# The expert scores of twelve turned columns: from twenty-four matmuls of 128 columns to six of 384

## The chip, the cores and the metric

The kernel runs on one core of one Trainium2 chip. The metric is the device time of one execution in microseconds, taken over repeated runs; the median of three is used. One further execution was recorded by the hardware profiler, and all rows below come from that one.

## What is computed

A sequence of 8 x 2880 tokens of width 192 goes through a short causal convolution with seven taps per head, whose weights are a softmax. Every token is then sent to one of 16 experts (4 groups of 4), a two-layer network with 1024 hidden units, and its output is scaled by the two softmax weights of the choice.

```python
w = softmax(weight_gen)                      # B, S, 8 heads, 7 taps
x = einsum('bshk,bskhg->bshg', w, windows(x_pad))
g_logits = x @ w_group                       # 4 groups
g_idx, g_w = argmax(g_logits), softmax(g_logits)[g_idx]
e_logits = x @ w_expert[g_idx]               # 4 experts of the group
e_idx, e_w = argmax(e_logits), softmax(e_logits)[e_idx]
h = maximum(x @ w1[g_idx, e_idx], 0)
out = g_w * e_w * (h @ w2[g_idx, e_idx])
```

The change concerns the logits alone: the product of every token with the 192 x 20 matrix of the 4 group weights and the 16 expert weights.

## The kernel before

The 23,040 tokens stand as 128 partitions by 180 columns; a *column* below is 128 tokens, one for each partition. The columns are worked in 15 groups of 12 (`WIDTHS`), and a group has two chunks of six. For each group VectorE computes the convolution (`conv`, L317 and L335; in the first six chunks TensorE adds up the products, L358). Then `logits` (L387) scores the group, `ranks` (L450) turns the scores into places in a table of rows, and GpSimd scatters the rows to DRAM (L527). Beside that, once rows are there, blocks of rows of one expert go through the two layers: `gemm1` (L965) and `gemm2` (L1011, later L1013 and L1014), and GpSimd scatters the results (L1049). One *unit* is one `gemm1` and one `gemm2` of an older unit.

The order on TensorE, ScalarE, VectorE and SyncE is the order of the program text as it is generated: a model of the engines' clocks (`clk`, `run`) decides when `step` takes the next piece of a group's work in between units. `run("pe", ...)` in `logits` is the model's cost of the scoring.

Inside `logits` the work of a group is this. Each pair of columns is turned by three transposes (L416, L417): the first 128 of the 192 features of each of the two columns, and the last 64 features of both, stacked on 128 partitions. ScalarE copies the three turned pieces, 384 columns, from PSUM to a tile `xT` (L423), one tile for each pair from a ring of six. `score` then handles two pairs, four token columns j = 0 to 3, with eight matmuls of 128 columns. Each column j has its own strip of 32 columns of the array and 32 partitions of the PSUM tile `lt` (`tile_position=(0, j * LW)`). The first four (u = 0) multiply the 128 features by `wr[:, 0]`, the second four (u = 1) add the product of the stacked 64 features with `wr[:, 1]` or `wr[:, 2]`, which hold the last 64 rows of the weights in the upper or the lower half of the partitions and zeros in the other.

In the groups before `FIRST` = 2 (`early`) a `score` follows each two pairs; from group 2 on all three follow one after another at the end, 24 matmuls. Then ScalarE copies `lt` to `lts` (L435), three transposes turn it back (L443), ScalarE copies the result to `ls` (L446), and `ranks` begins. The PSUM tile `pl` has one buffer, which `lt`, half of the transposes' outputs, `lp` and the ranks' sums use in turn.

Of the kernel before, what the change touches and what calls it, by code (L numbers as in the profile page):

```python
# [9 lines left out]
F32 = mybir.dt.float32  # L10
# [9 lines left out]
WIDTHS = (12,) * 15  # L20
# [22 lines left out]
def conv_moe_kernel(ctx: ExitStack, tc: tile.TileContext, x, wgen, w_group, w_expert, w1, w2, out):  # L43
    nc = tc.nc
# [4 lines left out]
    P = 128  # L49
# [3 lines left out]
    S = NTOK // P  # L53
    PB = P // B
    HALO = K - 1
    SG = 12
    SC = 6
# [14 lines left out]
    ENDS = [r[0] for r in ROUNDS]  # L72
    COL = [sum(WIDTHS[:g]) for g in range(len(WIDTHS) + 1)]
    CHUNK = [c // SC for c in COL]
    assert COL[-1] == S and ENDS[-1] == len(WIDTHS) and all(n % SC == 0 and n <= SG for n in WIDTHS)
    LAG = 2
    TB = 3

# [21 lines left out]
    rt = pool("rt", 1)  # L100
# [36 lines left out]
    ident = const.tile([P, P], F32, name="ident")  # L137
    make_identity(nc, ident)
    tri = const.tile([P, P], BF16, name="tri")
    LW = 32  # L140
    wr = const.tile([P, 3, LW], F32, name="wr")
# [23 lines left out]
    for n in (5, 4, 3, 2, 1):  # L165
        t = const.tile([P, NE], F32, name=f"first{n}")
# [15 lines left out]
    for n in sorted(set(WIDTHS)):  # L182
        t = smask[n] = const.tile([P, NE, n], F32, name=f"smask{n}")
# [70 lines left out]
    def ph_tile(k, shape):  # L254
        return ps_h.tile(shape, F32, name=f"ph{k}")
# [9 lines left out]
    def run(eng, cost, *deps):  # L265
        clk[eng] = max([clk[eng]] + [d + HOP for d in deps]) + cost
        return clk[eng]
# [119 lines left out]
    def logits(g, o):  # L387
        n = WIDTHS[g]
        xrow = o.xrow
        early = g < FIRST  # L390
        pause = lambda t: UNIT if state["begun"] and t > clk["pe"] + 0.9 else NEXT
        yield Chunk(o, 1)
        new_lt = lambda: ps_y.tile([P, SG // 4, P], F32, name="py0") if g == FIRST - 1 else ps_l.tile([P, SG // 4, P], F32, name="pl")
        lt = new_lt() if early else None

        def score(s4, xTs):
            for u in range(2):
                for j in range(2 * len(xTs)):
                    nc.tensor.matmul(  # L399
                        lt[j * LW:(j + 1) * LW, s4 // 4, :], lhsT=wr[:, u * (1 + j % 2), :], rhs=xTs[j // 2][:, (j % 2, 2)[u], :],  # L400
                        start=u == 0, stop=u == 1, tile_position=(0, j * LW))

        xTs, txTs = [], []
        for s2 in range(0, n, 2):
            if o.chunks <= s2 // SC:
                yield Chunk(o, s2 // SC + 1)
            if s2 % SC == 0:
                rem = rt.tile([P, SC, HP], F32, name="rem")
                nc.scalar.copy(out=rem, in_=xrow[s2 // SC][:, :, P:D])
                txTs += [run("act", 0.4, clk["dve"])] * 2  # L410
                yield pause(txTs[-1])
            ttp = run("pe", 0.35, txTs[-2])
            tp = ps_t.tile([P, 3, P], F32, name="tp") if s2 % 4 == 0 else ph_tile(0, [P, 3, P]) if early else ps_l.tile([P, SG // 4, P], F32, name="pl")
            row = xrow[s2 // SC][:, s2 % SC:s2 % SC + 2, :]
            for u in range(2):
                nc.tensor.transpose(out=tp[:, u, :], in_=row[:, u, 0:P], identity=ident)  # L416
            nc.tensor.transpose(out=tp[:, 2, :], in_=rem[:, s2 % SC:s2 % SC + 2, :].rearrange("p s d -> p (s d)"), identity=ident)  # L417
            if early and len(xTs) == 2:
                run("pe", 0.5, txTs[-1])
                score(s2 - 4, xTs)  # L420
                xTs = []
            xT = rt.tile([P, 3, P], F32, name="xT", bufs=SG // 2)
            nc.scalar.copy(out=xT, in_=tp)  # L423
            txTs.append(run("act", 0.48, ttp))
            xTs.append(xT)
            yield NEXT if s2 < n - 2 else pause(txTs[-1])
        lt = lt or new_lt()
        s4 = n - 2 * len(xTs)
        run("pe", 0.1 + 0.2 * len(xTs), txTs[-1])
        for i in range(0, len(xTs), 2):  # L430
            score(s4 + 2 * i, xTs[i:i + 2])
        lts = rt.tile([P, 3, P], F32, name="xT", bufs=SG // 2)
        lps = [(u, min(4, n - 4 * u) * LW) for u in range((n + 3) // 4)]
        if n % 4 == 0:
            nc.scalar.copy(out=lts[:, 0:n // 4, :], in_=lt[:, 0:n // 4, :])  # L435
        else:
            for u, w in lps:
                nc.scalar.copy(out=lts[0:w, u, :], in_=lt[0:w, u, :])
        tlt = run("act", 0.48, clk["pe"])
        yield pause(tlt)  # L440
        lp = ps_l.tile([P, SG // 4, P], F32, name="pl")
        for u, w in lps:
            nc.tensor.transpose(out=lp[:, u, 0:w], in_=lts[0:w, u, :], identity=ident[0:w, 0:w])  # L443
        run("pe", 0.35, tlt)
        ls = rt.tile([P, SG, NL], F32, name="ls")[:, 0:n, :]
        nc.scalar.copy(out=ls, in_=lp.rearrange("p q (j l) -> p (q j) l", l=LW)[:, 0:n, 0:NL])  # L446
        run("act", 0.4, clk["pe"])
        ranking.append([ranks(g, o, ls, Until(clk["act"] + LATE[0 if early else 1])), None])
# [230 lines left out]
    def front():  # L679
# [34 lines left out]
        for g in range(ENDS[-1]):  # L714
            o = grp[g]
            o.routed = False
            scoring.append([logits(g, o), None, o])
            for n, c in enumerate(conv(g, o)):
                yield c
                if g == 0 and n < 6:  # L720
                    for c in islice(rest, None if n == 5 else 1):
                        yield c
                if n == (2 if state["slots"] else 0) and 1 <= g < ENDS[-1] - 1:
                    load_group(g + 1)
                if n >= (12 if state["slots"] or g > FIRST else 4) and not o.ahead and g + 1 < ENDS[-1] and g != FIRST - 1:
                    o.ahead = True
                    side.append([softmax(g + 1), None])
                yield from beside(g, n)
                if g == FIRST - 1 and n in (7, 8):
                    if n == 7:  # L730
                        soft = softmax(FIRST)
                    yield next(soft)
            if g == FIRST - 1:
                for n, c in enumerate(soft):
                    yield c
                    yield from beside(g, n)
            yield from finish_all(side)
            if g:
                yield from settle(g - 1)
# [538 lines left out]
```

## Time and profile before

| | us |
|---|---|
| median of three runs | 1198.86 (1195.1 to 1199.44) |
| profiled execution | 1187.8 |
| its span, first to last instruction | 1185.8 |
| TensorE matmul busy | 1116.4 (94%), 8357 records |
| VectorE busy | 950.8 (80%) |
| ScalarE busy | 649.0 (55%) |
| GpSimd busy | 579.9 (49%) |

Busy time of TensorE is the time in which at least one matmul record is open; records overlap, and their ends are modelled. A matmul of this data type leaves two records, one for each pass, and each has a weight load of its own. "issue" as a reason for idle time means that the engine waited for nothing that the profile shows. In a timeline a row gathers neighbouring instructions of one kind: its start, the time to the end of the last one, their count, and in brackets the idle time ahead of it.

### The profile page before, as it was taken

The numbers are of one execution on the slowest core, as the hardware profiler recorded it, in microseconds if no ns is written. First come the engines' busy times: TensorE is split into PE (matmuls) and PEld (weight loads), VectorE is DVE, ScalarE is ACT, GpSimd is POOL, SyncE is SP. The second block draws the span as 40 slices with busy tenths as digits, with TensorE's granted clock in tenths as the row PEclk, the third lists the DMA queues.
The fourth block names the chain that finished last, engine by engine and source line by source line (L and its number), as shares of the span: only waits on it lengthen the run. The fifth ranks groups of instructions, "written<-read, shape, count | busy, mean of one in ns | idle before, by whom it ended". The sixth has DMA issues, their size and how long they took to land.

```text
span 1185.8 us, 24775 instructions
## 1 busy us (share of the span) xinstructions
PE 1116.4 (94%) x8357; PEld 1047.3 (88%) x8357; DVE 950.8 (80%) x1682; ACT 649.0 (55%) x1307; POOL 579.9 (49%) x613
## 2 busy tenths in 40 slices
PE   5787998999999999999999999999799899999997
PEld 2444988999999999998989999999799899999997
DVE  8899997989998989998988989898464576665661
ACT  1341435555565555665556566565446676666772
POOL 7164284647275745765563837284736421222221
PEclk9998999999999999999999999999999999999999
DMA  5798999887878777878795868767748875556562
GB/s 173 212 310 231 305 310 289 247 276 232 279 228 280 243 256 231 277 224 285 218 304 179 275 214 269 256 197 211 225 134 240 261 243 171 172 182 181 179 208 73
DMA packets 84345, 275.11 MB, mean 232 GB/s; under 512 B 15296, under 2 KB 34160, under 8 KB 82416
## 3 DMA queue, kind: packets, MB, share of 16 engines
q1 hardware_dynamic: 64056, 229.77, 62.3%
q0 software_dynamic: 20032, 43.39, 11.9%
q8 instruction: 67, 1.10, 0.4%
q14 instruction: 70, 0.57, 0.1%
q10 hardware_dynamic: 120, 0.28, 0.1%
HBM read 225.83 MB, written 47.88 MB: 231 GB/s over the span
## 4 chain that ended last, share of the span: by engine, by line
PE 65%; issue 15%; DVE 6%; DMA 4%; POOL 3%; ACT 3%; another core or an unknown queue 2%; SPq 0%; POOLq 0%; ACTq 0%; DVEq 0%
PE py L1011 27%; PE ph L965 27%; POOL out L1049 3%; DVE pr L317 3%; PE pl L399 2%; DMA raw<-in_moe_w 1%; PE tpx L940 1%; PE tpx L939 1%; PE ph L358 1%; PE py L1013 1%; DMA xb<-rows 1%; DVE pr L353 1%; PE tp L416 1%; PE pl L416 1%
## 5 line engine op out<-in xcount | busy, mean ns | idle before, releaser
L965 PE MATMUL ph<-xh,wa 128*128 128x256 f32 (+3 forms) x1992 | 455.0, 303 | 0.4 <-issue 0.3
L1049 POOL DMA_INDIRECT out<-y,xb x189 | 213.8, 1131 | 421.7 <-ACT y L1038 182.6
L1011 PE MATMUL py<-wc,hh 128*128 128x192 f32 x2160 | 400.9, 326 | 2.1 <-ACT y L1038 1.9
L965 PE MATMUL ph<-xl,wa 128*128 128x256 f32 (+3 forms) x1328 | 350.7, 285 | 1.0 <-DVE xl L896 0.6
L1011 PEld LDWEIGHTS py<-wc,hh 128*128 128x128 f32 x2160 | 345.5, 190 | 3.4 <-ACT y L1038 2.6
L965 PEld LDWEIGHTS ph<-xh,wa 128*128 128x128 f32 x1992 | 336.4, 190 | 6.5 <-issue 4.9
L974 ACT ACTIVATE hh<-ph 128x512 f32<-128x512 f32 (+2 forms) x296 | 165.8, 560 | 265.9 <-PE ph L965 233.2
L965 PEld LDWEIGHTS ph<-xl,wa 128*128 128x128 f32 x1328 | 251.6, 189 | 2.3 <-issue 1.1
L317 DVE TENSOR_TENSOR pr<-xin,wt 128x1152 f32<-128x1152 f32 x186 | 249.0, 1350 | 4.2 <-PE py L358 3.7
L527 POOL DMA_INDIRECT rows<-xrow,ix x156 | 222.2, 1425 | 47.3 <-POOL ix L526 32.9
L335 DVE TENSOR_TENSOR xrow<-xrow,pr 128x1152 f32<-128x1152 f32 x144 | 194.6, 1351 | 0.7
L896 DVE SCALAR_TENSOR_TENSOR pr<-ph,hh 128x256 fp32r<-128x256 f32 (+2 forms) x128 | 65.8, 514 | 87.4 <-ACT hh L979 44.3
L896 DVE TENSOR_TENSOR wa<-raw,wa 128x1024 fp32r<-128x1024 f32 x83 | 101.3, 1220 | 29.3 <-ACT wa L872 19.0
L526 POOL COPY ix<-posi 128x1 int32<-128x1 int32 x156 | 72.9, 479 | 73.3 <-DMA rows<-xrow,ix 39.2
L1013 PE MATMUL py<-wc,hh 128*128 128x384 f32 x320 | 101.8, 362 | 0.0
L979 ACT ACTIVATE hh<-ph 128x256 fp32r<-128x256 f32 (+2 forms) x128 | 59.1, 462 | 57.4 <-PE ph L965 55.2
L872 ACT CAST wa<-raw 128x1024 fp32r<-128x1024 f32 x83 | 87.2, 1050 | 0.0
L881 ACT CAST wa<-raw 128x1024 fp32r<-128x1024 f32 x83 | 86.5, 1043 | 0.0
L1014 PE MATMUL py<-wc,pr 128*128 128x192 f32 x320 | 80.5, 252 | 0.0
L1038 ACT ACTIVATE y<-py,xb 128x192 f32<-128x192 f32 x175 | 66.5, 426 | 20.5 <-PE py L1011 15.9
L896 DVE TENSOR_TENSOR xl<-tpx,xh 128x512 fp32r<-128x512 f32 (+1 forms) x92 | 59.2, 644 | 12.0 <-ACT xh L945 10.7
L1014 PEld LDWEIGHTS py<-wc,pr 128*128 128x128 f32 x320 | 61.5, 192 | 0.0
(205 smaller groups left out, 1341.6 us busy)
## 6 DMA issues: line engine op xcount, KB each, us to landing
wc<-in_moe_w SPq DMA_DIRECT2D x73, 768.0 KB
raw<-in_moe_w SPq DMA_DIRECT2D x83, 512.0 KB
xin<-in_x SPq DMA_DIRECT2D x14, 1728.0 KB
raw<-in_moe_w SPq DMA_DIRECT2D x91, 256.0 KB
raw<-w1lo SPq DMA_DIRECT2D x83, 256.0 KB
xb<-rows SPq DMA_DIRECT2D x75, 194.0 KB
wa<-in_moe_w SPq DMA_DIRECT2D x24, 384.0 KB
raw<-in_moe_w SPq DMA_DIRECT2D x11, 768.0 KB
```

The source lines that it names most:

```text
L317: nc.vector.tensor_tensor(out=dst, in0=o.xin[:, c0 + k:c0 + k + SC, :].rearrange("p s (h g) -> p s h g", g=HG), in1=w4[:, c0:c0 + SC, :, k ...
L335: nc.vector.tensor_tensor(out=acc, in0=acc, in1=prs[k - 2], op=ALU.add)
L527: written_once(nc.gpsimd.indirect_dma_start(out=rows[:, :], out_offset=bass.IndirectOffsetOnAxis(ap=ix, axis=0), in_=src, in_offset=None, ...
L872: nc.scalar.copy(out=o.wa[:, 0, :], in_=o.raw[0])
L881: nc.scalar.copy(out=o.wa[:, 2, :], in_=o.raw[1])
L896: f(*a, **k)
L965: nc.tensor.matmul(ph[:, v, :], lhsT=w[:, f0:f0 + P], rhs=rhs, start=i == 0, stop=i == len(terms) - 1)
L974: nc.scalar.activation(out=hh, in_=ph, func=AF.Relu)
L1011: nc.tensor.matmul(b.acc[t], lhsT=hh[:, v, c], rhs=wc[0][:, f, :], start=f == 0 and not (b.wide and t == 1), stop=f == NFT - 1 and not (b. ...
L1013: nc.tensor.matmul(b.py[t], lhsT=hh[:, v, c], rhs=wc[f // 4][:, f % 4].rearrange("p l d -> p (l d)"), start=f == 0, stop=False)
L1014: nc.tensor.matmul(b.acc[t], lhsT=hl[:, v, c], rhs=wc[f // 4][:, f % 4, 0, :], start=False, stop=f == NFT - 1)
L1049: ins = nc.gpsimd.indirect_dma_start(out=out[:, :], out_offset=bass.IndirectOffsetOnAxis(ap=b.x.bitcast(I32)[part, t, D + 1:D + 2], axis=0 ...
```

## The change

The six turned pairs of a group stand in one tile `xTs`, laid out by quarter of the group (four columns), pair and piece, in place of six tiles. `score(q0, q1)` takes quarters q0 to q1 at once, by an access pattern that steps over the quarters. The order of the two halves is turned round. First come two matmuls, one for each pair of the quarters, of the stacked 64 features with `wr[:, 1]` and `wr[:, 2]` side by side as 64 weight columns, so that one matmul gives both columns of a pair; they take strips of 64. Then come four matmuls in strips of 32 that add the 128 features' part. From group 2 on all three quarters go together, 384 columns for each matmul; in groups 0 and 1 a quarter at a time, 128 columns. `lts` becomes the first slice of `xTs`. The lines for groups whose width isn't twelve go; none has another width. The costs told to the clock model are the same.

```diff
--- before.py
+++ after.py
@@ -72,7 +72,7 @@
     ENDS = [r[0] for r in ROUNDS]
     COL = [sum(WIDTHS[:g]) for g in range(len(WIDTHS) + 1)]
     CHUNK = [c // SC for c in COL]
-    assert COL[-1] == S and ENDS[-1] == len(WIDTHS) and all(n % SC == 0 and n <= SG for n in WIDTHS)
+    assert COL[-1] == S and ENDS[-1] == len(WIDTHS) and all(n == SG for n in WIDTHS)
     LAG = 2
     TB = 3
 
@@ -393,14 +393,19 @@
         new_lt = lambda: ps_y.tile([P, SG // 4, P], F32, name="py0") if g == FIRST - 1 else ps_l.tile([P, SG // 4, P], F32, name="pl")
         lt = new_lt() if early else None
 
-        def score(s4, xTs):
-            for u in range(2):
-                for j in range(2 * len(xTs)):
-                    nc.tensor.matmul(
-                        lt[j * LW:(j + 1) * LW, s4 // 4, :], lhsT=wr[:, u * (1 + j % 2), :], rhs=xTs[j // 2][:, (j % 2, 2)[u], :],
-                        start=u == 0, stop=u == 1, tile_position=(0, j * LW))
-
-        xTs, txTs = [], []
+        xTs = rt.tile([P, SG // 4, 2, 3, P], F32, name="xT")
+
+        def score(q0, q1):
+            for w in range(2):
+                nc.tensor.matmul(
+                    lt[2 * w * LW:2 * (w + 1) * LW, q0:q1, :], lhsT=wr[:, 1:3, :].rearrange("p a l -> p (a l)"), rhs=xTs[:, q0:q1, w, 2, :],
+                    start=True, stop=False, tile_position=(0, 2 * w * LW))
+            for j in range(4):
+                nc.tensor.matmul(
+                    lt[j * LW:(j + 1) * LW, q0:q1, :], lhsT=wr[:, 0, :], rhs=xTs[:, q0:q1, j // 2, j % 2, :],
+                    start=False, stop=True, tile_position=(0, j * LW))
+
+        txTs, scored = [], 0
         for s2 in range(0, n, 2):
             if o.chunks <= s2 // SC:
                 yield Chunk(o, s2 // SC + 1)
@@ -415,32 +420,23 @@
             for u in range(2):
                 nc.tensor.transpose(out=tp[:, u, :], in_=row[:, u, 0:P], identity=ident)
             nc.tensor.transpose(out=tp[:, 2, :], in_=rem[:, s2 % SC:s2 % SC + 2, :].rearrange("p s d -> p (s d)"), identity=ident)
-            if early and len(xTs) == 2:
+            if early and s2 % 4 == 0 and s2:
                 run("pe", 0.5, txTs[-1])
-                score(s2 - 4, xTs)
-                xTs = []
-            xT = rt.tile([P, 3, P], F32, name="xT", bufs=SG // 2)
-            nc.scalar.copy(out=xT, in_=tp)
+                score(s2 // 4 - 1, s2 // 4)
+                scored = s2 // 4
+            nc.scalar.copy(out=xTs[:, s2 // 4, s2 % 4 // 2], in_=tp)
             txTs.append(run("act", 0.48, ttp))
-            xTs.append(xT)
             yield NEXT if s2 < n - 2 else pause(txTs[-1])
         lt = lt or new_lt()
-        s4 = n - 2 * len(xTs)
-        run("pe", 0.1 + 0.2 * len(xTs), txTs[-1])
-        for i in range(0, len(xTs), 2):
-            score(s4 + 2 * i, xTs[i:i + 2])
-        lts = rt.tile([P, 3, P], F32, name="xT", bufs=SG // 2)
-        lps = [(u, min(4, n - 4 * u) * LW) for u in range((n + 3) // 4)]
-        if n % 4 == 0:
-            nc.scalar.copy(out=lts[:, 0:n // 4, :], in_=lt[:, 0:n // 4, :])
-        else:
-            for u, w in lps:
-                nc.scalar.copy(out=lts[0:w, u, :], in_=lt[0:w, u, :])
+        run("pe", 0.1 + 0.4 * (n // 4 - scored), txTs[-1])
+        score(scored, n // 4)
+        lts = xTs[:, 0].rearrange("p w u t -> p (w u) t")[:, 0:3, :]
+        nc.scalar.copy(out=lts, in_=lt)
         tlt = run("act", 0.48, clk["pe"])
         yield pause(tlt)
         lp = ps_l.tile([P, SG // 4, P], F32, name="pl")
-        for u, w in lps:
-            nc.tensor.transpose(out=lp[:, u, 0:w], in_=lts[0:w, u, :], identity=ident[0:w, 0:w])
+        for u in range(n // 4):
+            nc.tensor.transpose(out=lp[:, u, :], in_=lts[:, u, :], identity=ident)
         run("pe", 0.35, tlt)
         ls = rt.tile([P, SG, NL], F32, name="ls")[:, 0:n, :]
         nc.scalar.copy(out=ls, in_=lp.rearrange("p q (j l) -> p (q j) l", l=LW)[:, 0:n, 0:NL])
```

TensorE, the group scored at 612 us in the profile: the end of a unit, the score, and the next unit (`pl` is the PSUM tile with the scores, `wr` the weights; a number behind a name is its buffer). Before:

```order
L1011 MATMUL py_7015<-wc,hh 128x192
L1011 MATMUL py_7016<-wc,hh 128x192
L399 MATMUL pl<-xT,wr 32x128 [waits Activation_49]
L399 MATMUL pl<-xT,wr 32x128 x23
L965 MATMUL ph_7089<-xh_181,wa 128x256 x2
L965 MATMUL ph_7089<-xl_183,wa 128x256 [waits DVE_49]
L965 MATMUL ph_7089<-xh_181,wa 128x256
```

And now:

```order
L1007 MATMUL py_6819<-wc,hh 128x192
L1007 MATMUL py_6820<-wc,hh 128x192
L400 MATMUL pl<-xT,wr 64x384 [waits Activation_49]
L400 MATMUL pl<-xT,wr 64x384
L404 MATMUL pl<-xT,wr 32x384 x4
L961 MATMUL ph_6873<-xh_181,wa 128x256 x2
L961 MATMUL ph_6873<-xl_183,wa 128x256 [waits DVE_49]
L961 MATMUL ph_6873<-xh_181,wa 128x256
```

The six matmuls stand where the twenty-four stood, behind the same unit, and the wait for ScalarE is on the first one in both.

TensorE, the second and the third quarter of group 0, behind its transposes. Before:

```order
L416 MATMUL tp<-ident,xrow 128x128 [waits PE_49]
L416 MATMUL tp<-ident,xrow 128x128
L417 MATMUL tp<-ident,rem 128x128
L399 MATMUL pl<-xT,wr 32x128 x2
L399 MATMUL pl<-xT,wr 32x128 [waits Activation_49]
L399 MATMUL pl<-xT,wr 32x128 x5
L416 MATMUL ph_380<-ident,xrow 128x128 [waits PE_49]
L416 MATMUL ph_380<-ident,xrow 128x128
L417 MATMUL ph_380<-ident,rem 128x128
L399 MATMUL pl<-xT,wr 32x128 [waits Activation_49]
L399 MATMUL pl<-xT,wr 32x128
```

And now:

```order
L421 MATMUL tp<-ident,xrow 128x128 [waits PE_49]
L421 MATMUL tp<-ident,xrow 128x128
L422 MATMUL tp<-ident,rem 128x128
L400 MATMUL pl<-xT,wr 64x128
L400 MATMUL pl<-xT,wr 64x128 [waits Activation_49]
L404 MATMUL pl<-xT,wr 32x128 x4
L421 MATMUL ph_372<-ident,xrow 128x128 [waits PE_49]
L421 MATMUL ph_372<-ident,xrow 128x128
L422 MATMUL ph_372<-ident,rem 128x128
```

Of the first score here the second pair's copy is waited for by the third of eight matmuls before, and by the second of six now. On the other four engines the order of the instructions, and which engines each waits for, is the same in both kernels.

## Rows read from the trace of the kernel before

**Rows 1.** stretch, length, busy us of PE, PEld, DVE, ACT, POOL, then clock, DMA, GB/s

```profile
20.00:120.00 100.00, 80.53 (x344) 44.87 (x342) 92.55 (x148) 31.43 (x60) 41.14 (x40) 0.93 0.80 232
...
300.00:500.00 200.00, 198.80 (x1612) 194.99 (x1611) 182.25 (x299) 117.25 (x220) 111.52 (x105) 1.00 0.79 251
500.00:850.00 350.00, 344.91 (x2685) 336.53 (x2683) 312.23 (x542) 202.76 (x383) 204.15 (x201) 1.00 0.76 240
```

**Rows 2.** the instructions of L399 (min/median/max ns) and its engine's idle time before them

```profile
L399 PE MATMUL pl<-xT,wr x672: 269/273/297, 35.3 to 854.5; 128*32 128x128 f32 x168
...
L399 PE MATMUL py<-xT,wr x48: 272/273/298, 65.5 to 80.1; 128*32 128x128 f32 x48
...
  issue: 13.8, 36
```

**Rows 3.** one group of L358, matmuls of 384 columns, ns

```profile
L358 PE MATMUL ph<-pr,ident x82: 485/486/979, 12.9 to 117.8; 128*128 128x384 f32 x82
```

**Rows 4.** timeline of TensorE, a score at 304 us: start, length, line, records

```profile
303.94 1.52 PE L399 MATMUL pl<-xT,wr 128*32 128x128 f32 x48
305.39 0.50 PE L965 MATMUL ph<-xh,wa 128*128 128x256 f32 x2
```

**Rows 5.** timeline of TensorE, L1022 with two strips of 64

```profile
1032.08 1.52 PE L1022 MATMUL pl<-xin,xrow 128*64 128x192 f32 x16
1033.53 0.56 PE L965 MATMUL ph<-xh,wa 128*128 128x320 f32 x2
```

**Rows 6.** timeline of TensorE, the score at 548 us

```profile
548.15 0.64 PE L399 MATMUL pl<-xT,wr 128*32 128x128 f32 x15
...
552.20 0.50 PE L965 MATMUL ph<-xh,wa 128*128 128x256 f32 x2
```

**Rows 7.** timeline of TensorE, the score at 426 us and behind it

```profile
426.41 1.92 PE L399 MATMUL pl<-xT,wr 128*32 128x128 f32 x47
...
428.88 0.78 PE L965 MATMUL ph<-xh,wa 128*128 128x256 f32 x2
...
431.13 0.27 PE L939 MATMUL tpx<-ident,xb 128*128 128x128 f32 x1
```

**Rows 8.** timeline of TensorE, the score at 612 us and behind it

```profile
611.88 1.50 PE L399 MATMUL pl<-xT,wr 128*32 128x128 f32 x42
...
615.10 0.49 PE L965 MATMUL ph<-xh,wa 128*128 128x256 f32 x2 [0.33 <-issue]
...
620.07 0.55 PE L443 MATMUL pl<-ident,xT 128*128 128x128 f32 x3 [1.48 <-ACT xT L435]
```

**Rows 9.** timeline of TensorE, the scores at 677 and 743 us

```profile
676.98 1.50 PE L399 MATMUL pl<-xT,wr 128*32 128x128 f32 x44
...
679.11 0.65 PE L965 MATMUL ph<-xh,wa 128*128 128x256 f32 x2
...
742.99 0.85 PE L399 MATMUL pl<-xT,wr 128*32 128x128 f32 x20
...
745.13 0.50 PE L965 MATMUL ph<-xh,wa 128*128 128x256 f32 x2
```

**Rows 10.** chain of waits, one ordinary unit: start, length, what

```profile
841.31 1.18 PE ph L965 x10
842.49 1.30 PE py L1011 x8
```

**Rows 11.** timeline of TensorE, the last score and behind it

```profile
851.53 1.68 PE L399 MATMUL pl<-xT,wr 128*32 128x128 f32 x41 [0.57 <-ACT xT L423]
...
860.04 0.90 PE L443 MATMUL pl<-ident,xT 128*128 128x128 f32 x3 [5.32 <-ACT xT L435]
...
862.87 1.55 PE L1011 MATMUL py<-wc,hh 128*128 128x192 f32 x8
```

**Rows 12.** busy time and granted clock behind the last score, columns as in group 1

```profile
860.00:862.90 2.90, 2.86 (x14) 2.86 (x15) 1.36 (x6) 0.36 (x1) 0.00 (x0) 0.50 0.00 0
```

**Rows 13.** timeline of TensorE, L443 behind a clean score

```profile
124.16 0.55 PE L443 MATMUL pl<-ident,xT 128*128 128x128 f32 x3 [0.60 <-ACT xT L435]
```


## Prediction

> **What bounds the kernel now.** I read the busy time by stretch first, then one line of code, then the timeline around it. Between 300 and 850 us TensorE is the engine without slack: busy 198.80 of 200 us and 344.91 of 350, while VectorE has 182.25 and 312.23 [rows 1]. At the start it is the other way round: from 20 to 120 us VectorE is busy 92.55 of 100 us and TensorE 80.53 [rows 1]. So a microsecond taken off TensorE after 300 us moves the end, and one taken off in the first 120 us mostly doesn't.
>
> The line of the change is the scoring, L399. Its 360 matmuls (13 scores of 24, and 6 of 8 in groups 0 and 1) appear as 672 + 48 = 720 records, two passes for each matmul, and each pass has a weight load of its own. The reader should see two things. A record lasts 273 ns, and TensorE sat idle before this line for 13.8 us, in 36 places, with "issue" as the reason: nothing that the profile shows was being waited for, the instructions were simply not there [rows 2].
>
> A clean score shows what the work itself costs. At 303.94 us 48 records start, and the next line starts at 305.39: 1.45 us [rows 4]. That is far less than 48 passes one after another, so the four strips of 32 columns run beside each other. A pass of 384 columns has a record of 486 ns [rows 3] and one of 128 columns 273 ns, so a column costs (486 - 273) / 256 = 0.83 ns, and 128 columns 0.107 us. Twelve rounds of four strips are 12 x 0.107 = 1.28 us; the other 0.17 us are the edges of the stretch.
>
> Of the ten scores after 300 us, six are not clean. From the first record to the next line they take 2.47 us at 426 [rows 7], 4.05 at 548 [rows 6], 3.22 at 612 [rows 8], 2.13 at 677 and 2.14 at 743 [rows 9], and the last, from its first record to the idle time ahead of L443, 860.04 - 5.32 - 851.53 = 3.19 against 1.52 in the clean one [rows 11, 4]. I read this as a queue that runs dry. An ordinary unit, 10 records of L965 in 1.18 us and 8 of L1011 in 1.30 [rows 10], has 18 matmul and 18 weight loads in 2.48 us, some 15 instructions per us. A clean score takes 96 instructions in 1.45 us, 66 per us.
>
> **The change part by part.** *Streaming.* Two matmuls of 64 weight columns and four of 32, each over 384 columns, are two rounds of two strips and two rounds of four: 4 x 384 x 0.83 ns = 1.28 us. The columns streamed fall from 24 x 128 to 6 x 384, but the time doesn't, since the old ones stood four abreast and the first two new ones stand only two abreast. Term: 0. That 64-wide strips do overlap in pairs is seen in L1022: 16 records of 192 columns take 1.45 us to the next line [rows 5]; one after another they would be 16 x 192 x 0.83 ns = 2.56 us.
>
> *The change of strip width.* Inside a score the array now goes from two strips of 64 to four of 32. No row shows that step. The nearest are the edges of a clean score and of L1022, which pass from and to the full width: 1.45 - 1.28 = 0.17 us in both [rows 4, 5]. [...] I take 0.17 for the 13 whole scores: +2.2 us. The six small ones lie before 85 us, beside the VectorE of rows 1; without that cover they would add 6 x 0.17 = 1.0 us. [...]
>
> *Instructions.* 720 records become 114 matmuls x 2 = 228, and in a whole score 96 instructions become 24, in 1.28 + 0.17 + 0.17 = 1.62 us: 15 per us, the rate of an ordinary unit, at which TensorE is not starved. So what the six scores have over the clean one should go: 1.02 + 2.60 + 1.77 + 0.68 + 0.69 + 1.67 = 8.4 us. Bounds: 0 (they come from something else) and 8.4; I take 8.4, as the four clean scores show that the work doesn't need them.
>
> *What follows a starved score.* After the one at 426 the next ten L965 take until 431.13, 2.25 us for 1.18: 1.07 lost [rows 7, 10]. After the one at 612, a unit and a wait for ScalarE's copy of the scores (L435) take from 615.10 to 620.07, 4.97 us for 2.48: 2.49 lost [rows 8, 10]. After the last one TensorE stands idle 5.32 us before L443, which waits for that copy, where a clean group has 0.60 [rows 11, 13]: 4.72 lost. [...] Together 9.7 us. These are not TensorE's instructions but the copy that comes late after them, in some starved groups and not in others, and one place has 6.1 of the 9.7. Bounds 0 and 9.7; I take half, 4.85.
>
> *Edits at nothing.* ScalarE makes the same copies of 384 columns, only into slices of one tile of the same total size; the order and the kinds of waits of VectorE, ScalarE, GpSimd and SyncE are unchanged, and no DMA is added. The one tile is reused by the next group, whose first copy must follow the L443 that read its first slice; but that copy already waits for transposes that stand behind L443 on TensorE, so no one waits longer. The first matmul of a whole score waited for the last copy before, too, since its sums lie in the bank that this copy frees. In groups 0 and 1 the second of the two wide matmuls waits for the second pair's copy, as the third of eight did.
>
> *Sum.* -8.4 - 4.85 + 2.2 = -11.1 us. The profiled execution took 1187.8 us (span 1185.8), which would become 1176.7. The median of the three runs is 1198.86, 11 us above the profiled one; I apply the difference to it: **1187.8**. With all that follows and a free change of width it is -8.4 - 9.7 = -18.1, 1180.8.
>
> **The rivals.** *A: the starved scores belong to the recorded execution.* The gaps lie where records come thickest, and the same work runs clean four times of ten. If timed runs have no such gaps, only the width step is left: 1198.9 to 1201.1, no change. For it: no row shows a resource that would hold instructions back. Against it: the profiled execution, with its gaps, is faster than all three timed ones, so recording didn't make it slow. [...]
>
> *B: the strips stop overlapping at 384 columns.* Then a score is 12 passes of 0.32 us and two edges, 3.84 + 0.34 = 4.18 us for 1.45: +2.73 x 13 = +35.5 us, less the 13.3 us of relief, +22: 1221, slower. It decides against the change from the point at which a score takes over 1.45 + 13.3/13 = 2.47 us. Against it: overlap holds in rows 4 at 128 columns and in rows 5 at 192, and nothing in either depends on the length.
>
> *C: VectorE takes the bound.* It is busy 91% and 89% of the two late stretches [rows 1]. TensorE's relief of 13 us in 550 is 2.4%, which would lift VectorE to about 93%. If its waits eat two thirds of the relief, 4.4 us are left, less 2.2 for the width: 1196.7, no change.
>
> **How the numbers follow.** Forecast 0.48, A 0.41, B 0.06, C 0.05. Half a per cent, 6 us, is about what a measurement of this kernel tells from no change; the forecast lies beyond it, from 1180 to 1193 in its own range, A and C within it, B on the slow side: faster 0.48, same 0.46, slower 0.06. Since forecast and A are near in weight, the range takes in both: from 1180 (everything goes) to 1202 (A with its width step and the spread of the runs). B is left out, with little of the edges of the other two.
>
> **What would show it.** In the profile of the changed kernel a whole score should take 1.45 to 1.65 us from its first record to the next line, in all ten late groups, and "issue" before the scoring lines should be near zero for its 13.8 us. Two records at a time should start in the first half of a score and four in the second; records that start 0.32 us apart one by one mean B. A gap of about 0.17 us between the halves confirms the width step. L443 of the last group should follow the copy by the 0.60 us of a clean one, and the clock should not fall to 0.50 there. If all this is seen and the timed runs stay at 1199, A is right, and my error is to have taken gaps of the record for gaps of the kernel. If the gaps merely move to L965 behind the score, the instruction rate wasn't the cause.

## The result, and the profile after

| us | before | after |
|---|---|---|
| median of timed runs | 1195.0 (1187.98 to 1199.44, six) | 1179.33 (1175.43 to 1183.13, six) |
| profiled execution, its span | 1187.8, 1185.8 | 1175.43, 1173.5 |
| TensorE busy, records | 1116.4 (94%), 8357 | 1110.5 (95%), 7865 |

The ratio of the medians is 0.9861 [0.9831, 0.9891] (the 95% interval stands in brackets behind a ratio): faster by 15.7 us. The forecast was 1187.8 with a range from 1180 to 1202; the time lies 0.7 us below the range. The sign was right, the size too small: 11.1 us forecast. The median of before rests on six runs here, the three shown ahead among them.

The timeline of TensorE in the changed kernel, the score at 612 us and the last one (start, length, line, records, idle time ahead):

```profile
611.76 0.87 PE L400 MATMUL pl<-xT,wr 128*64 128x384 f32 x4
612.55 0.85 PE L404 MATMUL pl<-xT,wr 128*32 128x384 f32 x8
613.34 0.50 PE L961 MATMUL ph<-xh,wa 128*128 128x256 f32 x2
...
844.88 0.87 PE L400 MATMUL pl<-xT,wr 128*64 128x384 f32 x4 [0.57 <-ACT xT L427]
845.67 0.85 PE L404 MATMUL pl<-xT,wr 128*32 128x384 f32 x8
847.13 0.55 PE L439 MATMUL pl<-ident,xT 128*128 128x128 f32 x3 [0.60 <-issue]
```

From its first record to the next line the score at 612 takes 1.58 us, where the old one took 3.22 [rows 8]; the other late scores take the same 1.58 us. Behind the last score L439 (L443 of before) comes 2.25 us after the score's start, with 0.60 us of idle time for the old 5.32 [rows 11].

The groups of TensorE's instructions (busy us, mean ns | idle before, and what ended it), first of before, then of the changed kernel, and for the latter the idle time by reason that belongs to L400 and then to L404:

```profile
L399 PE MATMUL pl<-xT,wr 128*32 128x128 f32 x672 | 27.2, 276 | 6.3 <-issue 3.6 <-ACT xT L423 2.5
L443 PE MATMUL pl<-ident,xT 128*128 128x128 f32 x45 | 8.2, 292 | 10.1 <-ACT xT L435 10.1
...
L400 PE MATMUL pl<-xT,wr 128*64 128x384 f32 (+1 forms) x64 | 13.3, 471 | 2.5 <-ACT xT L427 2.5
L404 PE MATMUL pl<-xT,wr 128*32 128x384 f32 (+1 forms) x128 | 12.4, 458 | 0.0
L439 PE MATMUL pl<-ident,xT 128*128 128x128 f32 x45 | 7.7, 280 | 4.7 <-ACT xT L434 4.1 <-issue 0.6
...
  issue: 2.6, 13
...
  issue: 8.8, 19
```

In the row of matmuls before had 3.6 us of "issue" ahead of the score. Now there is none: 0.0 us ahead of L404, and the 2.5 us ahead of L400 are ScalarE's copy, as they were. The wait ahead of the transposes behind the scores (L443, now L439) falls from 10.1 to 4.7 us. The second view still gives 2.6 + 8.8 us of "issue". It counts the weight loads' row too, and a load of 108 ns beside a record of 486 ns for 384 columns leaves that row idle between two loads (0.60 us ahead of L404's in the score at 612). In the same view the 13.8 us of [rows 2] hold the weight loads too, where the row of matmuls has 3.6; the row of matmuls alone is the one to read. Even that is less than the 8.4 us by which the six slow scores of before exceed a clean one, because an open record of 273 ns hides the start of each gap.

Busy time by stretch, columns as in [rows 1], the last behind L439:

```profile
300.00:500.00 200.00, 198.98 (x1470) 191.27 (x1469) 184.41 (x301) 116.75 (x218) 112.92 (x106) 1.00 0.79 248
500.00:850.00 350.00, 347.55 (x2552) 336.26 (x2551) 313.27 (x550) 206.47 (x389) 211.06 (x208) 1.00 0.79 246
847.10:850.00 2.90, 2.87 (x22) 2.88 (x23) 1.69 (x7) 0.96 (x2) 2.29 (x3) 1.00 0.94 358
```

TensorE still has the least slack. Behind the last score the clock is 1.00, where before it was at 0.50 [rows 12].

The two profiled spans differ by 12.3 us, and four stretches make that up. The first late score begins 1.41 us later than before (305.35 for 303.94 [rows 4]); from there to the last score's start the kernel takes 539.53 us for 547.59 (-8.06); from there to L439 2.25 for 8.51 (-6.26); from there to the end 326.37 for 325.76 (+0.61).

### The profile page after: what moved, and what is told of

Its sections match the earlier page's. It is cut to its first block, busy times and chain, and to the rows that moved or that the text cites. A ratio compares the mean times of both kernels' runs of the same rounds, so it can differ in the third digit from the quotient of the medians.

```text
span 1173.5 us, 23791 instructions
## 1 busy us (share of the span) xinstructions
PE 1110.5 (95%) x7865; PEld 1032.0 (88%) x7865; DVE 950.4 (81%) x1682; ACT 648.3 (55%) x1307; POOL 580.0 (49%) x613
## 3 DMA queue, kind: packets, MB, share of 16 engines
q8 instruction: 64, 1.05, 0.4%
## 4 chain that ended last, share of the span: by engine, by line
PE 55%; issue 20%; DVE 10%; DMA 6%; POOL 5%; ACT 2%; another core or an unknown queue 1%; POOLq 1%; SPq 0%; DVEq 0%; ACTq 0%
PE py L1007 25%; PE ph L961 22%; POOL out L1045 5%; DVE pr L317 4%; DMA xin<-in_x 2%; DVE xrow L335 1%; DMA raw<-in_moe_w 1%; PE tpx L936 1%; DMA xb<-rows 1%; PE tpx L935 1%; PE ph L358 1%; PE pl L404 1%; PE pl L400 1%; DMA rows<-rem 1%
```

## The experiments

In what follows, *before* and *the change* are the two kernels, a score *with gaps* is one whose records stop and start, and a ratio is a run's median over that of before on the same chip. The runs came in five groups, each on a chip of its own.

The theories. **Rate**: TensorE is held up where many of its instructions follow one another closely in one stretch, and the change helps because a score has 24 of them for 96. **Tile**: the one tile in place of six is what helps. **Wide**: the 64-wide strips are. **Count**, the rival of rate: each of the 24 matmuls costs something, wherever it stands. **Pair**: the gaps need GpSimd's scatters back to back at the same time. **Place**: how far instructions are held up is a property of the chip that the kernel runs on.

### One part of the change at a time

`e1_eight384`: one tile and 384 columns, but strips of 32 throughout, in the old order of the halves. Eight matmuls, 32 instructions a score.

```diff
-            for w in range(2):
-                nc.tensor.matmul(
-                    lt[2 * w * LW:2 * (w + 1) * LW, q0:q1, :], lhsT=wr[:, 1:3, :].rearrange("p a l -> p (a l)"), rhs=xTs[:, q0:q1, w, 2, :],
-                    start=True, stop=False, tile_position=(0, 2 * w * LW))
-            for j in range(4):
...
+            for u in range(2):
+                for j in range(4):
+                    nc.tensor.matmul(
+                        lt[j * LW:(j + 1) * LW, q0:q1, :], lhsT=wr[:, u * (1 + j % 2), :], rhs=xTs[:, q0:q1, j // 2, (j % 2, 2)[u], :],
+                        start=u == 0, stop=u == 1, tile_position=(0, j * LW))
```

> Scores as before in strips of 32, but with 384 columns: 8 matmuls, 32 instructions, no change of strip width. Theory 'rate' (the gain is that a score no longer takes 66 instructions per us): all ten late scores clean at 1.45 us to the next line, 'issue' before the scoring lines near zero, time 0.985 of before, some 1.5 us under the changed kernel, whose scores take 1.58. Rival 'wide' (the gain comes from the two halves' weights side by side, 2304 columns streamed for 3072): 1.00 of before. Rival 'tile' (the gain comes from the one tile): as 'rate'.

`e2_sixteen`: the same with two calls, of 256 and 128 columns: 64 instructions.

```diff
-        score(scored, n // 4)
+        for q0, q1 in ((scored, n // 4),) if early else ((0, 2), (2, 3)):
+            score(q0, q1)
```

> As the run with eight matmuls, but a late score in two parts of 256 and 128 columns: 16 matmuls, 64 instructions in some 1.45 us, 44 per us. 'Rate': some of the late scores starved, three or four of ten, with shorter gaps, 0.990 to 0.997 of before. 'Wide': 1.00. 'Tile': 0.985.

`e3_one_tile`: the same with three calls of 128 columns. These are the 24 matmuls of before, off one tile.

```diff
-        score(scored, n // 4)
+        for q in range(scored, n // 4):
+            score(q, q + 1)
```

> The one tile for the turned pairs alone: 24 matmuls of 128 columns in strips of 32, 96 instructions, as before. 'Rate' and 'wide': 1.00 of before, five to seven late scores starved. 'Tile': 0.985, all scores clean.

`e4_wide128`: the changed kernel with three calls of 128 columns (the same edit on it). 18 matmuls, 72 instructions, and the strip width changes five times in a score, where the changed kernel changes it once.

> The changed kernel's two wide and four narrow matmuls, but a quarter at a time: 18 matmuls of 128 columns, 72 instructions, with five more changes of strip width than the changed kernel. 'Rate': a clean score takes 1.58 + 5 x 0.13 = 2.2 us, 33 instructions per us; a few starved, 0.992 to 1.00 of before. 'Wide' and 'tile': a gain near that of the changed kernel, 0.986, less the 0.65 us a score, 0.992, and no starved score.

The four shared a chip, on which before took 1197.98 us:

| | instructions a score | ratio | late scores with gaps |
|---|---|---|---|
| e1, 8 x 384 | 32 | 0.9849 [0.980, 0.9898] | 0 of 10 |
| e2, 8 x 256 + 8 x 128 | 64 | 0.9962 [0.9931, 0.9994] | 1 |
| e4, 18 x 128, wide | 72 | 1.001 [0.9973, 1.0047] | 1 |
| e3, 24 x 128, one tile | 96 | 1.0018 [0.9985, 1.0051] | 7 |

TensorE's timeline: a score of e1, the last score of e2, and a score of e3.

```profile
546.68 1.50 PE L401 MATMUL pl<-xT,wr 128*32 128x384 f32 x16
548.11 0.50 PE L958 MATMUL ph<-xh,wa 128*128 128x256 f32 x2
```

```profile
852.91 1.51 PE L401 MATMUL pl<-xT,wr 128*32 128x256 f32 x32 [0.57 <-ACT xT L424]
857.84 0.90 PE L437 MATMUL pl<-ident,xT 128*128 128x128 f32 x3 [3.42 <-ACT xT L432]
```

```profile
616.05 1.66 PE L401 MATMUL pl<-xT,wr 128*32 128x128 f32 x38
618.09 0.38 PE L401 MATMUL pl<-xT,wr 128*32 128x128 f32 x3 [0.39 <-issue]
619.03 0.32 PE L401 MATMUL pl<-xT,wr 128*32 128x128 f32 x2 [0.56 <-issue]
619.78 0.43 PE L401 MATMUL pl<-xT,wr 128*32 128x128 f32 x3 [0.43 <-issue]
621.26 0.38 PE L401 MATMUL pl<-xT,wr 128*32 128x128 f32 x2 [1.05 <-issue]
621.57 0.82 PE L959 MATMUL ph<-xh,wa 128*128 128x256 f32 x2
```

In e1 the 16 records run in 1.43 us with no change of width. In e2 the 32 records run as closely, but ScalarE's copy behind them comes late, and L437 waits 3.42 us for it. In e3 the records come in clumps with nothing in between: the gaps of before. Tile falls with e3 (the whole layout, no gain), wide with e1 (no wide strip, all of the gain) and e4 (wide strips, none). The ratio goes with the number of instructions in a row, with one correction: a clean score of e4 takes 2.18 us for the changed kernel's 1.58, and 13 x 0.60 = 7.8 us, 0.65%, of its time are changes of width. e2 was expected to have three or four scores with gaps and has one. What it adds is that time is also lost behind the score, as a late copy, with no gap in the score itself: e4 has one score with gaps too, yet L440, the same transposes, waits 13.4 us in nine places, where the changed kernel's L439 waits 4.7.

### Whether GpSimd's scatters matter, and a spread score

`e5_gpsimd_spaced`: before, with small fills between GpSimd's scatters; `e6_eight_spaced` is the same edit on e1.

```diff
+        for _ in range(4):
+            nc.gpsimd.memset(idle, 0.0)
```

> The kernel before, with four small memsets on GpSimd ahead of each indirect store of results, so that these no longer start 1.28 us after each other (some 1.7 us). Theory 'pair' (a score of 96 instructions is starved, and ScalarE's copy behind it comes late, only where GpSimd's indirect DMAs stand one behind the other): fewer than three starved scores among ten, for six, and the copies' lag, 16 us in sum, under 8; 0.990 of before, if the stores themselves hold nothing up. Rival 'alone' (the rate of TensorE's instructions is enough by itself): as many starved scores as before, time 1.00 or a little slower.

> The same memsets in the kernel with eight matmuls of 384 columns. It shows what the memsets cost or give where there is no starved score. 'Pair': the copies' lag, 10 us in sum, falls too, and the time is that of the eight matmuls without memsets (0.985 of before) or up to 0.3% less. 'Alone': 0.985 to 0.990.

`e7_spread`: e3 with each quarter of a score behind a unit of its own, so that 32 instructions, not 96, follow one another (the last group's score and two quarters of another still stand together).

```diff
         for q in range(scored, n // 4):
+            if q > scored:
+                yield NEXT
             score(q, q + 1)
```

> 24 matmuls of 128 columns as before, off the one tile, but from group 2 on each quarter's eight matmuls behind a unit of its own (the last group and one quarter of another excepted): 32 instructions in a row in place of 96, the count over the kernel unchanged. 'Rate' (what counts is how many instructions come in a row): no starved score but perhaps the last group's, 0.985 to 0.990 of before. Rival 'count' (each of the 720 records costs something wherever it stands): 0.998 to 1.003.

Here before took 1167.98 us, 30 us less than on the chip of e1 to e4. The ratios are 1.0544 [1.0513, 1.0575], 1.0518 [1.05, 1.0535] and 1.0169 [1.013, 1.0208]. In time all three miss what either theory expected. None of the three has a score with gaps, and in e5 the scores are the 24 matmuls of before. The fills cost over 5% by themselves. The three tell nothing apart: with nothing held up, no edit can show what removes it, so pair was not tested. They raised the theory of place.

### The same on another chip

`e8_change_again` is the changed kernel, `e9_eight384_again` is e1 and `e10_spread_again` is e7, all unaltered.

> The changed kernel once more, beside the kernel before on one chip. In the last three runs the kernel before took 1168 us with a spread of 0.2%, and no score of 96 instructions was starved, while the five runs ahead of them had it at 1198 with a spread of 1.3%. Theory 'place' (how fast TensorE's instructions and signals get through differs from chip to chip, or by what runs beside): where before takes 1190 to 1200, the ratio is 0.986 again; where it takes some 1168, no score of either is starved, the change has only its step of strip width to show, 13 x 0.13 = 1.7 us, and the ratio is 1.000 to 1.003. Rival 'luck' (the last runs were short by chance): 0.986 whatever the time before.

> Eight matmuls of 384 columns in strips of 32, on the same chip. 'Place': 0.985 where before takes 1190 to 1200; where it takes some 1168, 0.998 to 1.001, and 0.1% under the changed kernel.

> 24 matmuls, but each quarter's eight behind a unit of its own. Where before takes some 1168 it was 1.017, as the longer way of the scores puts the later work off. Where before takes 1190 to 1200: by 'rate' no starved score but the last group's, and 1.017 less the 0.014 that starving costs, 1.00 to 1.005; by 'count' 1.017 again.

Before took 1170.84 us. The change: 1.0035 [1.0013, 1.0057]; e1's form: 1.0003 [0.9986, 1.0019]; spread: 1.0201 [1.0175, 1.0227]. The same change that had saved 1.4% costs a third of a per cent here, a little above the 1.000 to 1.003 expected.

### Before itself, on both kinds of chip

`e11_before_again` and `e13_before_third` are before, unaltered; `e12_spread_third`, beside e11, is e7, and `e14_change_third`, beside e13, is the changed kernel.

> The kernel before, profiled once more, for its own gaps beside the median of this chip. Theory 'place' (the 96 TensorE instructions in 1.45 us are held up on some chips and not on others, and the median of the kernel shows which kind it is): where its median is about 1195 us or more, at least half of the ten late scores take over 2 us and ScalarE's copies behind them lag by 10 us or more in sum; where it is about 1170, all ten take 1.4 to 1.5 us, the wait before L443 of the last group is 0.6 to 0.7 us, and the idle time with reason 'issue' before L399 is under 3 us. Rival 'kernel' (the gaps belong to every execution, and the medians differ for another reason): gaps as in the first profile, whatever the median.

> The 24 matmuls of 128 columns, each quarter behind a unit of its own, once more. Theory 'rate': on a chip on which the kernel before has its gaps this one has none or few, and is faster than before, ratio 0.985 to 0.995 by the scores, less what the two extra switches of a group cost; on a chip without gaps it is 1.7 to 2.0% slower as it was twice, by those switches alone. Rival 'count' (what is held up goes by the number of instructions, not by how closely they follow one another): scores with gaps here too wherever before has them, ratio 1.01 to 1.03 on either kind of chip.

> The kernel before, profiled a third time. Theory 'place': where its median is near 1170 us, all ten late scores take 1.4 to 1.5 us, ScalarE's copies behind them lag by 5 us or less in sum, and L443 of the last group waits 0.6 to 0.7 us; where it is near 1196, six or more take over 1.8 us and the copies lag by 15 us or more. Rival 'kernel': six or seven scores with gaps on either kind of chip, the 27 us between the medians lying elsewhere.

> The changed kernel beside it on the same chip. Theory 'place': ratio 0.983 to 0.990 where the kernel before has its gaps, 1.001 to 1.006 where it has none; its scores take 1.58 us in both. Rival 'kernel': the same ratio, about 0.986, on either kind of chip.

Beside e11 before took 1196.55 us, beside e13 1170.3. TensorE's timeline, first of e11, then of e13, at the score near 612 us and at the last:

```profile
614.89 1.66 PE L399 MATMUL pl<-xT,wr 128*32 128x128 f32 x40
616.94 0.39 PE L399 MATMUL pl<-xT,wr 128*32 128x128 f32 x3 [0.39 <-issue]
617.88 0.42 PE L399 MATMUL pl<-xT,wr 128*32 128x128 f32 x3 [0.55 <-issue]
618.65 0.39 PE L399 MATMUL pl<-xT,wr 128*32 128x128 f32 x2 [0.35 <-issue]
620.10 0.40 PE L965 MATMUL ph<-xh,wa 128*128 128x256 f32 x2 [1.05 <-issue]
...
867.43 0.90 PE L443 MATMUL pl<-ident,xT 128*128 128x128 f32 x3 [6.72 <-ACT xT L435]
```

```profile
612.09 1.52 PE L399 MATMUL pl<-xT,wr 128*32 128x128 f32 x48
613.54 0.50 PE L965 MATMUL ph<-xh,wa 128*128 128x256 f32 x2
...
844.57 1.52 PE L399 MATMUL pl<-xT,wr 128*32 128x128 f32 x48 [0.57 <-ACT xT L423]
846.68 0.55 PE L443 MATMUL pl<-ident,xT 128*128 128x128 f32 x3 [0.60 <-ACT xT L435]
```

The group of L399 in the two, again e11 first:

```profile
L399 PE MATMUL pl<-xT,wr 128*32 128x128 f32 x672 | 27.8, 276 | 8.5 <-issue 5.9 <-ACT xT L423 2.5
```

```profile
L399 PE MATMUL pl<-xT,wr 128*32 128x128 f32 x672 | 22.4, 275 | 2.5 <-ACT xT L423 2.5
```

It is one program, with the same 8357 TensorE records. In e11 seven of the ten late scores have gaps (six take 1.90 to 5.21 us, and the last one is the seventh); in e13 all ten run as one block, nine of them 1.45 us to the next line, and no time goes to "issue". Beside e13 the change gives 1.0007 [0.9988, 1.0026], just under the 1.001 to 1.006 expected: where before has no gaps there is nothing to win. So the gaps go with the median of the comparison, and the rival, gaps as in the first profile whatever the median, falls. That it is the chip itself, as place has it, is not shown: no chip came twice in the five groups, and what else ran there at the time isn't on record. Nor do the gaps account for the whole difference: the changed kernel takes 1179.33 us on the first chip and 1173.38 and 1172.84 on those without gaps. Those 6 us are not located.

Pair stays open, and the traces speak for it. GpSimd's scatters (start, length) around two scores of before, the one at 611.88, which has gaps, and the one at 802.27, which has none:

```profile
612.18 0.97 POOL L1049 DMA_INDIRECT out<-y,xb  x1 [0.30 <-ACT y L1038]
613.46 1.41 POOL L1049 DMA_INDIRECT out<-y,xb  x1 [0.30 <-issue]
...
801.02 1.67 POOL L527 DMA_INDIRECT rows<-xrow,ix  x1 [0.28 <-POOL ix L526]
803.00 1.94 POOL L1049 DMA_INDIRECT out<-y,xb  x1 [0.30 <-ACT y L1038]
```

In the three profiles of 96-instruction scores on chips with gaps (before, e3, e11) 20 of 30 late scores have gaps. All 20 have a scatter 0.97 or 0.98 us long that begins from 1 us ahead of the score's first record to 0.2 us behind it; none of the ten clean ones has. The last score of e12, 96 instructions in a row on such a chip, has neither. This was found in the traces afterwards, not expected ahead. Seven scores of e13 have such a scatter and no gap, so it isn't enough by itself. Whether the gaps need it was not tested on a chip that has them.

What comes late behind a score is seen on ScalarE, the copy of the last group's scores in e11 and in e13:

```profile
866.90 0.48 ACT L435 COPY xT<-pl 128x384 f32<-128x384 f32 x1 [9.09 <-remote]
```

```profile
846.15 0.48 ACT L435 COPY xT<-pl 128x384 f32<-128x384 f32 x1 [1.64 <-PE pl L399]
```

In e11 the last matmul of the score ends at 860.71 by its record, and ScalarE, idle all that time, starts the copy 6.19 us later; in e13 it is 0.07 us. The trace of e11 has the signal of TensorE's semaphore that the copy waits for at 866.88, so it was the signal that came late, not ScalarE. Since the ends of matmuls are modelled, a last matmul that finished late isn't excluded.

The spread score on the chip with gaps, TensorE's timeline:

```profile
630.78 0.64 PE L401 MATMUL pl<-xT,wr 128*32 128x128 f32 x16
631.36 0.50 PE L961 MATMUL ph<-xh,wa 128*128 128x256 f32 x2
...
636.49 0.65 PE L401 MATMUL pl<-xT,wr 128*32 128x128 f32 x16
637.06 0.50 PE L961 MATMUL ph<-xh,wa 128*128 128x256 f32 x2
```

From 300 us on no quarter and no score of e12 has a gap, with the same 24 matmuls of 128 columns. A quarter's 32 instructions take 0.58 us, 55 per us, nearly as closely as the 66 of a whole score. So what counts is how many follow closely in one stretch, not how many the kernel has, and not the rate alone: rate holds by the traces, its rival falls. As a time my expectation missed: 1.0107 [1.0061, 1.0152], where 0.985 to 0.995 was expected, and the time alone would fit the rival's 1.01 to 1.03. Against the 1.0169 and 1.0201 of the same kernel on chips without gaps it is 0.6 to 0.9% better. A score spread over three units comes late to the ranks and so to the rows: TensorE was busy 187.48 of the 200 us from 300 on (198.80 in before [rows 1]), and L935, which turns the rows of a block, waited 16.6 us for them, 4.0 in e11.

```profile
300.00:500.00 200.00, 187.48 (x1464) 181.56 (x1462) 176.43 (x285) 108.64 (x203) 95.31 (x94) 0.97 0.73 237
```

```profile
L935 PE MATMUL tpx<-ident,xb 128*128 128x128 f32 x175 | 45.1, 281 | 19.9 <-DMA xb<-rows 16.6 <-DVE xl L892 2.8 <-issue 0.5
```

```profile
L939 PE MATMUL tpx<-ident,xb 128*128 128x128 f32 x175 | 44.1, 276 | 7.7 <-DMA xb<-rows 4.0 <-DVE xl L896 3.3 <-issue 0.4
```

## Why the prediction was right, and where it was wrong

**The bound held, and the mechanism as far as it was needed.** TensorE was the engine to relieve, and a score of 24 instructions has no gap on either kind of chip. Removing the six slow scores (8.4 us) went as worked out. That the gaps are "a queue that runs dry", instructions that were simply not there, is not shown: "issue" says only that the profile shows nothing that was waited for. A late fetch of instructions isn't seen. The queue of the kind "instruction" whose packets fall with TensorE's instructions (q8, 67 packets before and 64 after) has 67 in e11 and in e13, at a median of 1.07 and 1.08 us, and none is under way in the slowest score of e11, at 614.89.

**The step that failed is "I take half"** of the 9.7 us that follow a slow score. The stretches of the first section show that most of it went. Between the first late score and L443, 8.06 + 6.26 = 14.3 us went; with 8.4 for the scores and ten width steps of 0.13 against it, 7.2 are left for this term, where half of it had been taken: of the 9.7 us 8.3 lie in that stretch, and half of those is 4.1. From the last score's start to L443 the whole is 1.67 + 4.72 us less the width step of 0.13, 6.26, and 6.26 was measured; by halves it would have been 3.9. Between 304 and 852 us the five other slow scores (6.76 us) and what follows two of them (3.56), less nine width steps (1.2), make 9.1; by halves it is 7.3, and 8.06 was measured. So the mis-sized part sits above all at the last group, in the 5.32 us before L443. I had halved it because the late copy was "not TensorE's instructions" and came in some starved groups only. e2, e4 and e11 show that the late copies go with the long stretch of instructions as the gaps do, in e2 and e4 behind scores that are clean themselves. So they belonged with the gaps, nearly whole (the changed kernel still waits 4.7 us at L439, 3.6 on chips without gaps): -8.4 - 9.7 + 2.2 = -15.9, against 15.7 measured between the medians. That these agree so closely is partly luck: the gaps differ from one execution to the next (six slow late scores in the first profile, seven in e11), the two profiled executions differ by 12.3 only, and the half clock is gone in the rows behind L439, yet the end didn't come sooner after it (+0.61). Its 1.42 us of the 9.7 are an estimate that no run shows, half of the 2.83 us from L443 to L1011 at a granted clock of 0.50 [rows 11, 12]; in its place the changed kernel showed 1.54 us for the same stretch (847.13 to 848.67) at a clock of 1.00, 1.29 less. It is luck too that the profiled execution took 1175.43 us, near the 1176.7 of the sum: the late copies gave back more than half, and the 1.41 us of later start and the 0.61 at the end took it away again.

**The base moved.** The sum was taken off 1198.86; with three more runs beside the changed kernel, before has 1195.0. Of the 8.5 us between forecast and result 3.9 are this, 4.6 the size of the gain. The lower end of the range, 1180.8 rounded to 1180, had everything go and a free change of width, but no room for the base: it missed by 0.7 us.

**The width step** was taken at 0.17 us, the edge of a clean score. It is 1.58 - 1.45 = 0.13 against e13's clean score, and 0.15 against e1; four more changes make a clean score of e4 2.18 - 1.58 = 0.60 us longer, 0.15 each. How much of it is the change itself and how much the load of 64 weight columns (134 ns for the 108 of 32) wasn't separated. The kernel that has no such change, e1, is the shorter one (1.43 us).

**The streaming term of zero** held: the half with two wide strips and the half with four narrow ones take 0.79 us each (611.76 to 612.55 to 613.34). B, strips that stop overlapping at 384 columns, is excluded by the rows at 612 us (1.58 us, not 4.18), C, VectorE as the bound, by TensorE's 198.98 of 200 us.

**Rival A** was wrong in its result and half right in its reason. I argued that gaps belong either to the kernel or to the recorded execution. They belong to neither alone: in three comparisons before takes 1195 to 1198 us, and both of its profiles from these have gaps; in three it takes 1168 to 1171, and its one profile has none. On the second kind the change gave 1.0035 and 1.0007, which is no change by the bound of the forecast. The timed runs have a granted clock on record as well, so none of them is known to be free of records, and that recording itself holds TensorE up was neither shown nor excluded. For it: on chips with gaps the traces hold fewer of TensorE's signals than on the others (878 and 873 in two profiles of before, 951 in e13), and fewer landings of DMAs (11523 and 11223, 15114 in e13). Against it as the whole cause: e12 lacks as many (871) and none of its scores from 300 us on has a gap. With signals missing, the reasons that the views of those chips give for a wait ("issue", "remote") are the less certain. Why a long stretch is held up on one chip and not on another stays open.

**The check that was set badly**: "issue" before the scoring lines "near zero" was read from a view that counts the weight loads, where the changed kernel has 11.4 us and even e13, without a gap, 2.6.

**Which version is best.** e1's form, eight matmuls of 384 columns off one tile with the strips left at 32, gains as much where there are gaps (0.9849 [0.980, 0.9898], the change 0.9861 [0.9831, 0.9891]; the runs don't tell them apart) and costs nothing where there are none (1.0003, the change 1.0035 on the same chip). The wide strips save eight instructions of 32 and pay the width step for it.

## What to carry to other kernels

Count how many instructions a stretch takes one behind another, and how closely: 96 in 1.45 us were held up here on some chips, 32 in 1.43 or in 0.58 us were not, and longer moving operands lower the count without streaming less. Count what waits behind such a stretch (in before a late copy, with 5.32 us of idle time, and a clock of 0.50 [rows 11, 12]) with it. Before betting on a gap with the reason "issue", look for it on more than one chip, for what is won back on one may never have been lost on another.

## What the hardware showed that was not expected

- One program, unaltered, takes 1195 to 1198 us on some chips and 1168 to 1171 on others, and the profiles of the slower kind have gaps between TensorE's instructions: 5.9 us of "issue" ahead of L399's matmuls in e11, none in e13.
- In e11 ScalarE's copy, which waits for TensorE's signal, started 6.19 us after the last matmul had ended by its record (0.07 us in e13); TensorE stood idle for 6.72 us over it.
- Four strips of 32 columns run beside each other at 384 columns as they do at 128: 16 records of 486 ns in 1.43 us, 48 of 273 ns in 1.45.
